# The opening of a fused attention and feed-forward kernel: 64 by 64 tiles, full rows for the last tokens' keys, shorter norms, another order

## The chip, the cores and the metric

The kernel runs on one core of one Trainium2 chip. A core has a matrix engine (PE, with its weight loads PEld), a vector engine (DVE), an activation engine (ACT), a general engine (POOL) and a sync engine (SP), whose queue here issues nearly all the transfers. The engines run their own instruction queues in order and wait for each other by semaphores. Matrix products land in PSUM; everything else that is worked on lies in SBUF. The metric is the device time of one execution in microseconds (us), the median over the runs.

## The reference

```python
# q, k, v: (8 batches, 8 heads, 576 tokens, 64), g_norm: (64,)
kv = np.einsum('bhsd,bhse->bhde', k, v)
out = np.einsum('bhsd,bhde->bhse', q, kv)
rms = np.sqrt(np.mean(out * out, axis=-1, keepdims=True) + 1e-06)
attn = (out / rms * g_norm).astype(np.float32)
x = np.ascontiguousarray(attn.transpose(0, 2, 1, 3)).reshape(4608, 512)
h = x @ w_in                      # w_in (512, 2048)
r = np.maximum(h, 0.0)
out = ((r * r) @ w_out)           # w_out (2048, 512)
```

Per head a 64 by 64 matrix kv is summed over all 576 tokens; each token's query is multiplied by it, normalised over its 64 numbers and scaled by g_norm. The eight heads of a token make one row of 512 numbers, which goes through two weight matrices with a squared relu between them. The weights arrive as 64-bit floating point numbers and are turned into 32-bit ones on the chip.

## The kernel before

**Tiling.** Heads are taken in pairs p (four of them for each batch b), so that two times 64 numbers fill 128 partitions. Of a head's 576 tokens, 512 make four full chunks of 128 rows, and the last 64 ("rest") are held for all heads in `k_rest` and `v_rest`, in rows 0 to 63 for an even batch and 64 to 127 for an odd one (`load_rest`, L159 to L163). The feed-forward works on nine strips of four 128-token tiles. Strip 0 is multiplied plainly, strip 1 with seven products in place of eight, the strips from 2 on with that scheme two levels deep; the sums of weights that the schemes need are built on DVE, stored to device memory and read back (`w_deep<-w_t`, `w_blk<-w_deep`).

**Weights.** They come in 32 pieces of 512 KB (`raw`, eight buffers, issued by SP at L240). A piece is converted by ACT's absolute value of the high words (L254), ACT's scaling of the low words (L258) and four steps (`conversion`): clamp (L266), shift (L268), combine (L272), add into the weights (L275). All four are DVE's, but for the first step of pieces 1, 2 and 3, which POOL does. From piece 4 on, pieces are converted in twos between the products of strip 0 (`convert_pieces`).

**The opening.** Batch 0's first four tiles are worked pair by pair in an order that is written out by hand in the list `slices` (L692 to L703). Each entry is one call, and every engine takes its instructions in the order of these calls. The letters are:
- T, `transposed_query` (L381): for batch 0, eight products with the identity (L407) put a pair's query on its other side in PSUM; ACT copies them to `qT` (L409). Ahead of the first, `keep_busy` (L376 to L379) issues products that nobody reads.
- K, `key_value` (L418): for each head of the pair four products over full chunks and one over the rest's 64 rows (L435), then two ACT copies of the 64 by 64 results into a block matrix `kv_all` (L440, L441).
- Q, `first_queries` (L582): four 128 by 128 products with the block matrix (L585), ACT's Square (L480), DVE's sum over 64 numbers (L488) and DVE's scaling by 1/64 plus epsilon (L489).
- N, `first_normalized` (L588): ACT's root (L494), DVE's reciprocal (L499), three small steps that sharpen the inverse root (L501 to L503), and DVE's multiplication into `x_n` (L592).
- F, `first_features` (L607): four transposes on PE (L611), and an ACT copy to the strip's `xT`, scaled by g (L612).
- U, `first_up` (L616): products of a pair's features with the first weights (L622); pair p needs piece p.
- size and low, the ACT steps L254 and L258 of a piece; piece, some of its four later steps.

The PSUM of the opening is the pool `apsum` (L99), two buffers for each tag: "at" for T and K, "first" for Q. The pool is replaced when strip 0 begins. SP's queue holds, in this order, batch 0's q, k, v and rest, with raw pieces between, then raw pieces to the eighth, batch 1's first keys, values, queries and rest, then raw pieces as their buffers come free.

**After the opening** the rest of strip 0 follows, with two pieces converted between its products. The remaining slices are called as the strips' products go on.

Of the kernel before, what the change touches and what calls it, by code (L numbers as in the profile page):

```python
# [10 lines left out]
FP32 = mybir.dt.float32  # L11
# [3 lines left out]
AF = mybir.ActivationFunctionType  # L15
ALU = mybir.AluOpType
AX = mybir.AxisListType
# [3 lines left out]
def kernel(  # L21
# [74 lines left out]
    psums = ExitStack()  # L96
    fpsum = psums.enter_context(tc.tile_pool(name="fpsum", bufs=4, space=bass.MemoryType.PSUM))
    opening = ExitStack()
    apsum = opening.enter_context(tc.tile_pool(name="opsum", bufs=2, space=bass.MemoryType.PSUM))  # L99
    ctx.enter_context(tc.manual_schedule())  # L100


# [54 lines left out]
    squares = lambda t: t.rearrange("p h d -> p (h d)").rearrange("p (k q f) -> p k q f", k=4, f=SQ)  # L157

    def load_rest(b, eng):  # L159
        h = b % 2  # L160
        half = slice(REST * h, REST * (h + 1))
        for t, src in ((k_rest[half], k), (v_rest[half], v)):
            eng.dma_start(out=t, in_=src[b, :, C * P : S].rearrange("h s d -> s h d"))  # L163
# [179 lines left out]

    kv_all = const.tile([P, 2 * NP, P], FP32, name="kv_all")
    nc.gpsimd.memset(kv_all, 0.0)

    one = const.tile([P, 1], FP32, name="one")
    nc.vector.memset(one, 1.0)
    nc.scalar.sqrt(one, one)

    load_next()
# [9 lines left out]
    g_src = g_norm.rearrange("(d u) -> d u", u=1)  # L361
    for h in range(2):
        nc.scalar.dma_start(out=g_col[ts(h, D)], in_=g_src)


    qT, kvd, x_n, xt = {}, {}, {}, {}
# [8 lines left out]
    def keep_busy(ps, n):  # L375


        for _ in range(n):
            nc.tensor.matmul(ps, lhsT=ident, rhs=ident[:, : ps.shape[1]], start=True, stop=True)  # L379

    def transposed_query(b, p):  # L381
        while any(f == load and a[:2] == (b, p) for f, a in drips):
            drip()
        t = main.pop(("q", b, p))
        if b >= Q_ON_PE:
            qT[b, p] = qt_pool.tile([P, C, P], FP32, name="qT", tag="qT")
            nc.vector.transpose(out=flat(qT[b, p]), in_=flat(t))
            if b % 2 and p == NP - 1:
                while any(f == load_q_rest and a[0] <= b for f, a in (*rest_drips, *drips)):
                    drip(not drips)  # L390
                nc.vector.transpose(
                    out=open_rest(b).rearrange("p q (k t) -> p q k t", k=4),
                    in_=squares(q_rest[b // 2]).rearrange("p k q f -> p q k f"),
                )
            drip_queries()
            if p == NP - 1 and b + 1 < B:
                (rest_drips, drips)[b % 2 == 0].extend((load_q_rest, (b + 1, nc.sync, a)) for a in range(4))
            return
        ps = apsum.tile([P, C, P], FP32, name="t_ps", tag="at")
        if (b, p) == (0, 0):  # L400
            keep_busy(ps[:, 0], 7)
        for c in range(C):
            if b:
                nc.tensor.transpose(ps[:, c, :], flat(t[:, c]), ident)
                continue
            for h in range(2):
                nc.tensor.matmul(ps[ts(h, D), c, :], lhsT=t[:, h, c], rhs=ident, start=True, stop=True)  # L407
        qT[b, p] = qt_pool.tile([P, C, P], FP32, name="qT", tag="qT")
        nc.scalar.copy(qT[b, p], ps)  # L409
        if (b, p) == (1, NP - 1):  # L410
            drip_queries()
# [6 lines left out]
    def key_value(b, *ps_of):  # L418
        while any(f == load and a[:2] == (b, p) or f == load_rest and a[0] == b for _, f, a in keys_due for p in ps_of):
            _, f, a = keys_due.popleft()  # L420
            f(*a)
        ps = apsum.tile([P, len(ps_of), D], FP32, name="kv_ps", tag="at")
        if (b, ps_of[0]) == (0, 0):
            keep_busy(ps[:, 0], 3)
            warm = apsum.tile([P, NT, P], FP32, name="x_ps", tag="first")[:, 0]
        half = slice(REST * (b % 2), REST * (b % 2 + 1))
        tiles = [[main.pop((n, b, p)) for n in "kv"] for p in ps_of]
        steps = [(i, c) for i in range(len(ps_of)) for c in range(C)] + [(i, C) for i in range(len(ps_of))]
        for i, c in steps:
            if (b, ps_of[i], c) == (0, 0, C):  # L430
                keep_busy(warm, 2)
            for h in range(2):
                at = (slice(None), h, c) if c < C else (half, 2 * ps_of[i] + h)
                a, w = (t[at] for t in (tiles[i] if c < C else (k_rest, v_rest)))
                nc.tensor.matmul(  # L435
                    ps[ts(h, D), i], lhsT=a, rhs=w, start=i == 0 and c == 0, stop=c == C, skip_group_check=True
                )
        at = (NP * b + ps_of[0]) % (2 * NP)
        d = kv_all[:, at : at + len(ps_of)]
        nc.scalar.copy(d[0:D, :, 0:D], ps[0:D])  # L440
        nc.scalar.copy(d[D:P, :, D:P], ps[D:P])  # L441
        for i, p in enumerate(ps_of):
            kvd[b, p] = d[:, i]
            if b < 2:
                if b == 1 and p == 0:
                    load_next()
            else:
                u = next(to_load, None)
                if u is not None:
                    keys_later(load, *u, nc.sync, "kv")  # L450
                if p == (1 if b > 3 else NP - 1) and b + 1 < B:
                    keys_later(load_rest, b + 1, nc.sync)
# [23 lines left out]
    def squared_parts(parts, pool=xn_pool, tag="x_n"):  # L476
        sqs = []
        for ps in parts:
            sqs.append(pool.tile(list(ps.shape), FP32, name="sq", tag=tag))
            nc.scalar.activation(sqs[-1], ps, AF.Square)  # L480
        return sqs

    def mean_of(sqs):
        ms = small.tile([P, 2, H], FP32, name="ms", tag="ms")[:, : len(sqs)]
        for i, sq in enumerate(sqs):
            if len(sq.shape) == 3:
                sq = sq.rearrange("p r e -> p (r e)")
            nc.vector.reduce_sum(out=ms[:, i], in_=by_head(sq), axis=AX.X)  # L488
        nc.vector.tensor_scalar(out=ms, in0=ms, scalar1=1.0 / D, scalar2=EPS, op0=ALU.mult, op1=ALU.add)  # L489
        return ms  # L490
# [6 lines left out]
    def inverse_root(ms, r):  # L497
        t = small.tile([P, 2, H], FP32, name="newton", tag="newton")[:, : ms.shape[1]]
        nc.vector.reciprocal(r, r)  # L499

        nc.vector.scalar_tensor_tensor(out=t, in0=ms, scalar=-0.5, in1=r, op0=ALU.mult, op1=ALU.mult)  # L501
        nc.vector.tensor_tensor(out=t, in0=t, in1=r, op=ALU.mult)
        nc.vector.scalar_tensor_tensor(out=t, in0=t, scalar=1.5, in1=r, op0=ALU.add, op1=ALU.mult)  # L503
        return t
# [75 lines left out]


    def first_queries(p):  # L582
        ps = apsum.tile([P, NT, P], FP32, name="x_ps", tag="first")
        for n in range(NT):
            nc.tensor.matmul(ps[:, n, :], lhsT=qT[0, p][:, n, :], rhs=kvd[0, p], start=True, stop=True)  # L585
        first[p] = flat(ps), mean_of(squared_parts([flat(ps)]))

    def first_normalized(p):  # L588
        ps, ms = first.pop(p)
        x_n["first", p] = t = xn_pool.tile([P, NT, P], FP32, name="x_n", tag="x_n")  # L590
        r = inverse_root(ms, root_of(ms))[:, 0]
        nc.vector.tensor_tensor(  # L592
            out=by_head(flat(t)), in0=by_head(ps), in1=r.unsqueeze(2).to_broadcast([P, H, D]), op=ALU.mult
        )

    first_steps = {}
# [10 lines left out]
    def first_features(p):  # L607
        t, x = x_n.pop(("first", p)), open_xt(0)
        ps = fpsum.tile([P, NT, P], FP32, name="xt_ps", tag="f")
        for n in range(NT):  # L610
            nc.tensor.transpose(ps[:, n, :], t[:, n, :], ident)  # L611
        nc.scalar.activation(x[:, :, p, :], flat(ps).rearrange("p (a t) -> p a t", t=SQ), AF.Copy, scale=g_col)  # L612

    first_sums = {}

# [76 lines left out]
    act, T, K, Q, N, F, piece = (  # L692
        convert_on_act, transposed_query, key_value, first_queries, first_normalized, first_features, first_piece
    )
    U = first_up
    size, low = (lambda i: (act, (i, (0,)))), (lambda i: (act, (i, (1,))))
    slices += [(T, (0, 0)), (K, (0, 0)), (T, (0, 1)), (Q, (0,)), (K, (0, 1)), (N, (0,)), size(0), (piece, (0, 1))]
    slices += [(T, (0, 2)), (Q, (1,)), low(0), (piece, (0, 1)), (K, (0, 2)), (N, (1,)), (F, (0,)), (T, (0, 3))]
    slices += [(piece, (0, 1)), (Q, (2,)), (piece, (0, 1)), size(1), (K, (0, 3)), low(1), (N, (2,)), (F, (1,))]
    slices += [(piece, (1, 4)), (Q, (3,)), size(2), low(2), (U, (0, [0, 1, 2])), size(3), (F, (2,)), (piece, (2, 4))]  # L700
    slices += [(U, (1, [0, 1, 2])), (N, (3,)), low(3), (piece, (3, 4)), (U, (2, [0, 1])), (F, (3,)), (U, (2, [2]))]
    slices += [(U, (3, [0, 1, 2]))]
    ready[0] = len(slices)  # L703
    def query_pairs(b):
        first_n = b // 2 * PAIR + (C if b % 2 else 0)
# [791 lines left out]
```

## Time and profile before

| What | Value |
|---|---|
| median of 3 runs | 870.81 us (870.48 to 872.5) |
| the profiled execution's own time | 869.32 us |
| its span, first to last instruction | 867.5 us |
| granted PE clock | 1.00 |
| PE busy | 860.8 us (99%) |
| DVE busy | 720.3 us (83%) |
| ACT busy | 352.2 us (41%) |
| POOL busy | 315.2 us (36%) |
| chain that ended last, by engine | PE 83%, DVE 9%, ACT 3%, DMA 3%, issue 2% |

A busy share is an average over stages that differ. The windows over the first 50 us show how the start differs from the rest: time, busy time of the engines (number of instructions), granted clock, share and rate of the DMA engines.

```profile
0.00:5.00 5.00, 3.64 (x18) 3.41 (x20) 0.06 (x1) 1.49 (x2) 1.60 (x7) 1.00 0.56 167
5.00:10.00 5.00, 5.00 (x60) 4.35 (x58) 0.00 (x0) 1.00 (x3) 0.00 (x0) 1.00 1.07 282
10.00:15.00 5.00, 5.00 (x76) 4.21 (x74) 2.41 (x8) 3.53 (x9) 0.00 (x0) 1.00 1.06 384
15.00:20.00 5.00, 4.71 (x59) 3.83 (x59) 4.54 (x13) 4.24 (x12) 0.75 (x1) 1.00 1.06 403
20.00:25.00 5.00, 4.63 (x20) 2.66 (x20) 4.65 (x12) 4.04 (x8) 3.84 (x3) 1.00 1.07 393
25.00:30.00 5.00, 5.00 (x15) 2.01 (x13) 4.45 (x12) 1.33 (x3) 1.13 (x1) 1.00 0.82 205
```

The columns behind the window and its length are PE, PEld, DVE, ACT and POOL. DVE does nothing before 12 us, since the first sums need q, k, v and the rest to have landed (q of pair 0 at 3.52, k 4.50, v 5.83, k_rest 7.41, v_rest 8.15 us). The DMA engines are saturated from 5 to 25 us. PE is called busy while a product waits in it, so its 5.00 doesn't mean that it was at its peak.

### The profile page before, as it was taken

How to read it: one execution, taken by the hardware profiler on the slowest of the kernel's cores; microseconds unless marked ns; L12 is line 12 of the kernel's file. 1: busy time of each engine (PE TensorE's matmuls, PEld its weight loads, DVE VectorE, ACT ScalarE, POOL GpSimd, SP SyncE). 2: the span in 40 equal slices, each digit the busy share in tenths (PEclk: the TensorE clock that was granted, in tenths of full speed). 3: DMA queues.
4: the chain of work that ended last, by engine and by line, in shares of the span. 5: the costliest groups of instructions: out<-in, count | busy, mean ns of one | idle time of the engine just before them, and what ended most of it. 6: DMA issues, size and time to landing. Idle time of an engine off the chain costs nothing.

```text
span 867.5 us, 32585 instructions
## 1 busy us (share of the span) xinstructions
PE 860.8 (99%) x14176; PEld 805.7 (93%) x14176; DVE 720.3 (83%) x1236; ACT 352.2 (41%) x805; POOL 315.2 (36%) x319
## 2 busy tenths in 40 slices
PE   9999999999999999999999999999999999999998
PEld 7445888889999999999999999999999999999998
DVE  3999998879877996789689977897889777976887
ACT  5799251320048403750356034901491148102810
POOL 1100004630459323730574045704470447145700
PEclk9999999999999999999999999999999999999999
DMA  9998997999999997989688979997668856875483
GB/s 317 302 339 251 279 376 229 285 325 374 290 256 262 343 319 230 238 311 335 211 244 272 341 240 265 287 311 268 210 223 301 303 168 215 294 283 195 173 313 126
DMA packets 169470, 236.47 MB, mean 273 GB/s; under 512 B 78704, under 2 KB 133744, under 8 KB 161008
## 3 DMA queue, kind: packets, MB, share of 16 engines
q1 hardware_dynamic: 169024, 234.33, 83.5%
q8 instruction: 111, 1.82, 0.9%
q14 instruction: 31, 0.25, 0.1%
q10 hardware_dynamic: 304, 0.07, 0.0%
HBM read 197.66 MB, written 36.70 MB: 270 GB/s over the span
## 4 chain that ended last, share of the span: by engine, by line
PE 83%; DVE 9%; ACT 3%; DMA 3%; issue 2%; SPq 0%; DVEq 0%; ACTq 0%
PE ps_A L852 36%; PE ps_B L852 32%; PE ps_C L852 5%; PE ps_A L857 4%; PE kv_ps L435 2%; DVE w_c L272 2%; PE x_ps L471 2%; PE ps_B L857 2%; DVE w_t L292 1%; DMA w_deep<-w_t 1%; DVE wt L292 1%; DMA first_qkv<-in_v_dram 1%; DVE w_c L266 1%; PE ps_C L857 1%; DVE w_in L275 1%
## 5 line engine op out<-in xcount | busy, mean ns | idle before, releaser
L852 PE MATMUL ps_B<-w_blk,g_s 128*64 128x128 f32 x2016 | 121.8, 273 | 0.0
L852 PEld LDWEIGHTS ps_B<-w_blk,g_s 128*64 128x64 f32 x2016 | 112.4, 137 | 0.1
L852 PE MATMUL ps_A<-x_l,w_in 128*64 128x128 f32 x1568 | 102.8, 273 | 0.7 <-ACT snap L1315 0.6
L292 POOL TENSOR_TENSOR x_l<-xT 128x256 f32<-128x256 f32 x21 | 16.1, 765 | 228.6 <-PE ps_A L852 228.6
L852 PE MATMUL ps_B<-w_blk,gt 128*64 128x128 f32 x1504 | 93.9, 273 | 0.0
L852 PE MATMUL ps_A<-w_blk,g_s 128*64 128x128 f32 x1536 | 92.0, 273 | 0.0
L852 PEld LDWEIGHTS ps_A<-x_l,w_in 128*64 128x64 f32 x1568 | 89.0, 137 | 0.9 <-ACT snap L1315 0.8
L1310 POOL TENSOR_TENSOR snap<-snap,gt 128x512 f32<-128x512 f32 x35 | 46.3, 1322 | 113.4 <-ACT snap L1315 104.1
L852 PEld LDWEIGHTS ps_A<-w_blk,g_s 128*64 128x64 f32 x1536 | 85.5, 137 | 0.0
L852 PEld LDWEIGHTS ps_B<-w_blk,gt 128*64 128x64 f32 x1504 | 84.4, 137 | 0.3 <-issue 0.3
L1315 ACT COPY snap<-ps_A 128x512 f32<-128x512 f32 x63 | 36.9, 585 | 103.6 <-PE ps_A L852 94.4
L1250 ACT ACTIVATE gt<-gt 128x512 f32<-128x512 f32 x112 | 70.1, 626 | 8.8 <-DVE gt L1310 8.8
L1251 ACT ACTIVATE gt<-gt 128x512 f32<-128x512 f32 x112 | 70.7, 631 | 3.6
L852 PE MATMUL ps_A<-w_blk,gt 128*64 128x128 f32 x1152 | 71.0, 273 | 0.0
L1099 ACT COPY o_sb<-ps_A 128x128 f32<-128x128 f32 x24 | 6.4, 266 | 144.9 <-PE ps_A L852 115.4
L852 PEld LDWEIGHTS ps_A<-w_blk,gt 128*64 128x64 f32 x1152 | 64.5, 137 | 0.0
L292 DVE TENSOR_TENSOR gt<-gt 128x2048 f32<-128x2048 f32 (+1 forms) x29 | 59.7, 2063 | 0.0
L1098 DVE TENSOR_TENSOR o_sb<-o_sb,ps_B 128x256 f32<-128x256 f32 (+1 forms) x123 | 47.5, 386 | 14.5 <-ACT o_sb L1099 9.4
L1310 POOL TENSOR_TENSOR gt<-gt,snap 128x512 f32<-128x512 f32 x42 | 52.6, 1282 | 14.9 <-DVE snap L1310 14.9
L852 PE MATMUL ps_B<-x_l,w_blk 128*64 128x128 f32 x784 | 51.4, 273 | 0.0
L852 PE MATMUL ps_A<-x_l,w_blk 128*64 128x128 f32 x784 | 51.2, 273 | 0.0
L1099 ACT COPY o_sb<-ps_B 128x128 f32<-128x128 f32 x31 | 8.2, 266 | 96.3 <-PE ps_B L852 96.3
(194 smaller groups left out, 1838.1 us busy)
## 6 DMA issues: line engine op xcount, KB each, us to landing
w_blk<-w_deep SPq DMA_DIRECT2D x56, 1024.0 KB, 7.2
w_blk<-w_out SPq DMA_DIRECT2D x56, 768.0 KB, 6.5
w_blk<-w_in_deep SPq DMA_DIRECT2D x49, 768.0 KB, 6.0
raw<-in_moe_w_in_dram SPq DMA_DIRECT2D x16, 512.0 KB, 7.8
raw<-in_moe_w_out_dram SPq DMA_DIRECT2D x16, 512.0 KB, 5.2
k<-in_k_dram SPq DMA_DIRECT2D x29, 256.0 KB, 5.1
v<-in_v_dram SPq DMA_DIRECT2D x29, 256.0 KB, 5.3
x_d<-x_q SPq DMA_DIRECT2D x27, 256.0 KB, 4.9
```

The lines of the kernel that those rows point to most:

```text
L272: yield nc.vector.scalar_tensor_tensor(out=ci, in0=high, scalar=-(2**30), in1=ci, op0=ALU.bitwise_and, op1=ALU.bitwise_or)
L292: eng.tensor_tensor(out=out, in0=a, in1=b, op=ALU.subtract)
L435: nc.tensor.matmul(ps[ts(h, D), i], lhsT=a, rhs=w, start=i == 0 and c == 0, stop=c == C, skip_group_check=True)
L471: nc.tensor.matmul(ps[half, r, i, ts(p, D)], lhsT=q[row, half], rhs=kvd[b, p][row, row], start=True, stop=True)
L852: nc.tensor.matmul(ps[half], lhsT=lhsT[:, half], rhs=rhs, start=start, stop=stop, skip_group_check=True)
L857: nc.tensor.matmul(bank[BANK[p]][:, i, :], lhsT=lhsT(k), rhs=rhs(k), start=p in (1, 5, 2) and i == 0 and k == 0, stop=k == n - 1, skip_gro ...
L1098: add = lambda out, a, b: nc.vector.tensor_tensor(out=out, in0=a, in1=b, op=ALU.add)
L1099: yield nc.scalar.copy(q[:, 3:4], small(1))
L1250: nc.scalar.activation(o, o, AF.Relu)
L1251: nc.scalar.activation(o, o, AF.Square)
L1310: add = lambda eng, out, a, b: eng.tensor_tensor(out=out, in0=a, in1=b, op=ALU.add)
L1315: nc.scalar.copy(t, ps)
```

## The change

- The queries of batch 0 are transposed in 16 products of 64 by 64 tiles for each pair (new function `first_transposed`), and multiplied in 16 products of 64 by 64 tiles without the zero blocks.
- The opening's PSUM pool has one buffer. Two tiles are taken once and kept for all four pairs: "t" of two by two blocks of 256 columns, in which T uses blocks [:, :, 0] and K 64 columns of block [:, p % 2, 1], and "x", in which pair p of Q uses [:, :, p % 2]. The warm-up products write in "x", and there are 6, 1 and 2 of them for 7, 3 and 2.
- `k_rest` and `v_rest` of batches 0 to 3 lie in rows 0 to 63; rows 64 to 127 are set to zero, and the products of K go over all 128 rows. `load_rest` of batches 1, 2 and 3 thus writes the rows that the batch before has read.
- The norm: Square gets the scale 64^-0.5, the root gets epsilon as its bias, the step L489 is gone, and the sharpening steps give -2 times the inverse root, which the factor -0.5 in `g_neg` undoes. The root is a step R of its own.
- The order in `slices` is another one.

```diff
-    apsum = opening.enter_context(tc.tile_pool(name="opsum", bufs=2, space=bass.MemoryType.PSUM))
+    apsum = opening.enter_context(tc.tile_pool(name="opsum", bufs=1, space=bass.MemoryType.PSUM))
...
     def load_rest(b, eng):
-        h = b % 2
+        h = b % 2 * (b > Q_ON_PE + 1)
...
+    for t in (k_rest, v_rest):
+        nc.gpsimd.memset(t[REST:P], 0.0)
...
+    eps = const.tile([P, 1], FP32, name="eps")
+    nc.vector.memset(eps, EPS)
...
+    g_neg = const.tile([P, 1], FP32, name="g_neg")
+    nc.gpsimd.tensor_scalar(out=g_neg, in0=g_col, scalar1=-0.5, scalar2=None, op0=ALU.mult)
...
+    def first_transposed(p):
+        t = main.pop(("q", 0, p))
+        if p == 0:
+            open_ps["t"] = apsum.tile([P, 2, 2, C * D], FP32, name="t_ps", tag="t")
+            open_ps["x"] = apsum.tile([P, 2, 2, NT * D], FP32, name="x_ps", tag="x")
+            keep_busy(open_ps["x"][:, 0, 1, 0:P], 6)
+        ps = open_ps["t"][:, :, 0]
+        for c in range(C):
+            for s in range(2):
+                rows = slice(REST * s, REST * (s + 1))
+                for h in range(2):
+                    nc.tensor.matmul(
+                        ps[ts(h, D), s, ts(c, REST)], lhsT=t[rows, h, c], rhs=ident[rows, rows], start=True, stop=True
+                    )
+        qT[0, p] = qt_pool.tile([P, C, P], FP32, name="qT", tag="qT")
+        nc.scalar.copy(
+            qT[0, p].rearrange("p c (s t) -> p s c t", s=2), ps.rearrange("p s (c t) -> p s c t", t=REST)
+        )
...
     def transposed_query(b, p):
+        if b == 0:
+            return first_transposed(p)
...
-        if (b, p) == (0, 0):
-            keep_busy(ps[:, 0], 7)
         for c in range(C):
-            if b:
-                nc.tensor.transpose(ps[:, c, :], flat(t[:, c]), ident)
-                continue
-            for h in range(2):
-                nc.tensor.matmul(ps[ts(h, D), c, :], lhsT=t[:, h, c], rhs=ident, start=True, stop=True)
+            nc.tensor.transpose(ps[:, c, :], flat(t[:, c]), ident)
...
-        ps = apsum.tile([P, len(ps_of), D], FP32, name="kv_ps", tag="at")
+        if b:
+            ps = apsum.tile([P, len(ps_of), D], FP32, name="kv_ps", tag="at")
+        else:
+            ps = open_ps["t"][:, ps_of[0] % 2, 1, 0:D].rearrange("p (i d) -> p i d", i=1)
+            warm = open_ps["x"][:, 0, 1, 0:P]
         if (b, ps_of[0]) == (0, 0):
-            keep_busy(ps[:, 0], 3)
-            warm = apsum.tile([P, NT, P], FP32, name="x_ps", tag="first")[:, 0]
-        half = slice(REST * (b % 2), REST * (b % 2 + 1))
+            keep_busy(warm, 1)
+        half = slice(REST * (b % 2), REST * (b % 2 + 1)) if b > Q_ON_PE + 1 else slice(None)
...
     def first_queries(p):
-        ps = apsum.tile([P, NT, P], FP32, name="x_ps", tag="first")
+        ps = open_ps["x"][:, :, p % 2]
         for n in range(NT):
-            nc.tensor.matmul(ps[:, n, :], lhsT=qT[0, p][:, n, :], rhs=kvd[0, p], start=True, stop=True)
-        first[p] = flat(ps), mean_of(squared_parts([flat(ps)]))
+            for h in range(2):
+                half = slice(REST * h, REST * (h + 1))
+                for r in range(2):
+                    row = slice(D * r, D * (r + 1))
+                    nc.tensor.matmul(
+                        ps[half, r, ts(n, D)], lhsT=qT[0, p][row, n, half], rhs=kvd[0, p][row, row], start=True, stop=True
+                    )
+        sq = xn_pool.tile([P, 2, NT * D], FP32, name="sq", tag="x_n")
+        nc.scalar.activation(sq, ps, AF.Square, scale=D**-0.5)
+        ms = small.tile([P, 2, H], FP32, name="ms", tag="ms")[:, 0]
+        nc.vector.reduce_sum(out=ms, in_=sq.rearrange("p r (n d) -> p (r n) d", d=D), axis=AX.X)
+        first[p] = ps, ms
+
+    def first_root(p):
+        r = small.tile([P, 2, H], FP32, name="rms", tag="rms")[:, 0]
+        nc.scalar.activation(r, first[p][1], AF.Sqrt, bias=eps)
+        first[p] += (r,)
 
     def first_normalized(p):
-        ps, ms = first.pop(p)
+        ps, ms, r = first.pop(p)
...
-        r = inverse_root(ms, root_of(ms))[:, 0]
+        w = small.tile([P, 2, H], FP32, name="newton", tag="newton")[:, 0]
+        nc.vector.reciprocal(r, r)
+        nc.vector.scalar_tensor_tensor(out=w, in0=ms, scalar=EPS, in1=r, op0=ALU.add, op1=ALU.mult)
+        nc.vector.tensor_tensor(out=w, in0=w, in1=r, op=ALU.mult)
+        nc.vector.scalar_tensor_tensor(out=w, in0=w, scalar=-3.0, in1=r, op0=ALU.add, op1=ALU.mult)
...
-        nc.scalar.activation(x[:, :, p, :], flat(ps).rearrange("p (a t) -> p a t", t=SQ), AF.Copy, scale=g_col)
+        nc.scalar.activation(x[:, :, p, :], flat(ps).rearrange("p (a t) -> p a t", t=SQ), AF.Copy, scale=g_neg)
...
-    slices += [(T, (0, 0)), (K, (0, 0)), (T, (0, 1)), (Q, (0,)), (K, (0, 1)), (N, (0,)), size(0), (piece, (0, 1))]
-    slices += [(T, (0, 2)), (Q, (1,)), low(0), (piece, (0, 1)), (K, (0, 2)), (N, (1,)), (F, (0,)), (T, (0, 3))]
-    slices += [(piece, (0, 1)), (Q, (2,)), (piece, (0, 1)), size(1), (K, (0, 3)), low(1), (N, (2,)), (F, (1,))]
-    slices += [(piece, (1, 4)), (Q, (3,)), size(2), low(2), (U, (0, [0, 1, 2])), size(3), (F, (2,)), (piece, (2, 4))]
-    slices += [(U, (1, [0, 1, 2])), (N, (3,)), low(3), (piece, (3, 4)), (U, (2, [0, 1])), (F, (3,)), (U, (2, [2]))]
-    slices += [(U, (3, [0, 1, 2]))]
+    slices += [(T, (0, 0)), (K, (0, 0)), (T, (0, 1)), (Q, (0,)), (K, (0, 1)), (R, (0,)), (T, (0, 2)), (N, (0,)), (Q, (1,))]
+    slices += [size(0), (R, (1,)), (piece, (0, 1)), low(0), (piece, (0, 3)), (N, (1,)), (F, (0,)), (K, (0, 2))]
+    slices += [(T, (0, 3)), (Q, (2,)), size(1), low(1), (piece, (1, 1)), (R, (2,)), (N, (2,)), (U, (0, [0, 1, 2])), (F, (1,))]
+    slices += [(K, (0, 3)), size(2), (piece, (2, 1)), (piece, (1, 3)), (F, (2,)), (Q, (3,)), (R, (3,)), low(2)]
+    slices += [(U, (1, [0, 1, 2])), (piece, (2, 3)), size(3), (piece, (3, 1)), low(3), (N, (3,)), (U, (2, [0, 1]))]
+    slices += [(F, (3,)), (piece, (3, 3)), (U, (2, [2])), (U, (3, [0, 1, 2]))]
```

In the last two lists `(piece, (i, n))` calls for the next n of the four steps of piece i.

## The prediction

> **What bounds the kernel now.** Four views, each narrowing the last. The slices show PE at 90% or more nearly everywhere, but DVE at 9 from the second slice to the sixth (21.7 to 130 us), in which PE is busy too.
>
> ```profile
> PE   9999999999999999999999999999999999999998
> ...
> DVE  3999998879877996789689977897889777976887
> ```
>
> The chain of work that ended last settles which of the two binds: from 42.2 to 107 us each of its pieces but short issue gaps is DVE's, then comes `107.16 8.56 DMA w_deep<-w_t`, then DVE again to 130.94, and only from 131.60 is it PE to the end. So the opening's share of the time is decided by when DVE's unbroken run of conversions begins. The same chain, taken to 32 us, shows how it begins now:
>
> ```profile
> 29.00 0.45 PE xt_ps L611 x4
> 29.45 0.02 issue
> 29.47 0.69 ACT xT L612
> 30.16 0.55 ACT w_c L254
> ```
>
> F(3), the transposition of the last pair's features, ends in an ACT copy at 29.47; only behind it does ACT take piece 4 (L254). The timeline of DVE shows what that delays:
>
> ```profile
> 27.71 0.69 DVE L592 TENSOR_TENSOR x_n<-x_ps,newton 128x512 f32<-128x512 f32 x1
> ...
> 29.60 0.69 DVE L275 CUSTOM_DVE_ANT_0 w_in<-raw,w_c 128x1024 uint16<-128x1024 uint16 x1
> 30.74 0.43 DVE L266 TENSOR_SCALAR w_c<-w_c 128x512 f32<-128x512 f32 x1 [0.45 <-ACT w_c L254]
> 31.87 0.43 DVE L266 TENSOR_SCALAR w_c<-w_c 128x512 f32<-128x512 f32 x1 [0.70 <-ACT w_c L254]
> ```
>
> After 32.2 us DVE has no idle time of weight before 98 us: the windows give 5.00 of 5.00 us for 35 to 40, 20.00 of 20.00 for 40 to 60 and for 60 to 80, 19.97 for 80 to 100. Hence my measure: **the start of DVE's L266 of piece 5, now 31.87 us.** A later start passes on one for one, for DVE's queue behind it is full, the store w_deep<-w_t follows DVE, and PE's final run at 131.60 follows that store (its last wait is for a w_deep landing at 131.57). An earlier start is capped: on ACT, L254 waited for raw pieces at 48.21 (0.83 us) and 51.05 (0.40 us); they landed at 48.13 and 50.96, behind DMA engines at shares of 0.99 to 1.11 since 35 us. DVE takes them some 1.4 to 1.8 us later, and no more than that can be gained.
>
> **Parts that shorten something.** Durations are rows of the profiled execution, from its groups by line and its timeline.
> - Transposes T: a group now takes 1.09 us (9.21 to 10.31, L407). The nearest row for 16 tiles of 64x64 is products_x's L471, 0.69 us at 142.16. Bounds: 0.33 us (four records of the rest's 64x64 tiles, L435) and 1.09. I take 0.65, between the two readings 0.62 and 0.69 of L471.
> - Products Q: 1.16 us now (L585), same nearest row, same bounds with 1.16 on top; 0.65.
> - The rest of the keys in full rows: 0.33 us now; the chunk rows of L435 are 0.69 for 16 records, so 0.17 for four. The two POOL memsets are half of L345's 128x1024 each or less (0.95 us), so they end by 3.2 us; K0's rest needs them at 8.15, v_rest's landing. K0's rest begins at 8.96 now, behind warm-up matmuls (L379, 8.31); with fewer of these it can begin at 8.2.
> - Norms: L489 goes from each of the four chains, 0.17 us each (12.79 of pair 0; 0.53 for pair 2, under contention). The scale moves into Square, EPS into Sqrt's bias, the factor -0.5 to g_neg, which one POOL instruction prepares with POOL idle from 2.2 to 19.25. Square with a scale has no row here; between nothing and one L480's slack I take nothing. The eps memset (0.06 us) lies before DVE's first work at 12.07.
>
> **Part that adds waits.** apsum goes from two buffers to one, and T, K on the one hand and Q on the other share one tile each through the whole opening. From the waits that the changed program's instructions carry I read: K(p) waits for the ACT copy of T(p); T(p+1) for ACT's two kv copies of K(p); Q(p+1) for DVE's x_n of N(p); Q(2) and Q(3) likewise. None of these is there now: Q of pair 1 runs 13.23 to 14.39 while x_n of pair 0 runs 14.15 to 14.84, and Q of pair 2 begins at 16.80, ahead of x_n of pair 1 at 17.16. So what ran a pair ahead becomes one chain. Worked out with rows, 0.05 us from engine to engine:
>
> - v_rest 8.15; K0's rest to 8.5; kv copies 2 x 0.21, 9.0; T1 9.05; Q0 9.5 to 10.15; Square 0.60, 10.8; reduce 0.69, 11.55; root behind K1's copies 11.8; reciprocal to x_n's start 0.92 as at 13.23; **x_n of pair 0 at 12.8**, 1.35 earlier than now.
> - Q1 must wait for it to end: 13.5 (now 13.23). Square to 14.8, reduce to 15.5. The new order then has all of piece 0 ahead of N1: 0.42 + 0.42 + 0.69 + 0.69, the third held by L258 on ACT to 16.5: 17.8. Three newton steps, **x_n of pair 1 at 18.65** (now 17.16).
> - Q2 19.4 (now 16.80), Square to 20.7, reduce 21.4, root behind L258 21.9, **x_n of pair 2 at 22.9** (now 21.43).
> - PE: U(0), three products of 0.86, runs from 19.9 to 22.4; F1, K3, F2 follow, Q3 at 24.4 (now 19.72); Square behind F2's copy 25.3 to 25.9; reduce 26.6. Piece 2's L268 waits for POOL's L266 (1.92 us from 24.85), L272, L275 to 28.8. **x_n of pair 3 at 29.6** (now 27.71).
> - F3 behind U(2) at 30.5; ACT's copy 31.2 (now 29.47); L254 of piece 4 at 31.8; of piece 5, and with it DVE's L266, **33.65 (now 31.87): 1.8 us later.**
>
> What hides elsewhere: SP's queue keeps its order, but load_rest of batch 1 now reuses rows 0 to 63 and waits for K3, at about 23.6 instead of its issue at 22.85. Behind it stand two k/v loads, two q loads and raw 8; the transfer issued at 22.85 lands 7.62 us later, so the DMA engines have more queued than the 0.75 us; without that cover it would cost 0.75. The raw buffers 10 and 11 hang on pieces 2 and 3 ending at 28.8 and 32.1 (now 26.9 and 30.3): issues now at 30.59 and 31.48, so the latter slips 0.7; DVE needs it 1.8 later as well.
>
> **The sum.** The profiled execution took 869.32 us, 867.5 of span and 1.8 around it. 867.5 + 1.8 + 1.8 = 871.1. The median of the runs shown is 870.81, 1.5 above; on that footing **872.6 us**. Bounds of the unknown: T and Q at their old lengths add 0.5 at Q2 and 0.5 at F3's end, +1.0; at 0.33 us they give back 0.3 at each of Q1, Q2 and Q3, -0.9. So 871.7 to 873.6 for the row part, and 870.9 to 874.6 with the one to one passage uncertain by 1 us.
>
> A rule that bears on the waits: the Trainium skill, page "PSUM — Partial Sum Buffer", section "PSUM bank collisions raise a hardware error", says that two engines in one bank and one quarter of the partitions collide, and that a dependency is set between them even at other columns. By it the two halves of a shared tile, which lie in the same banks, must wait for each other, as in the waits above; without it Q1 would run ahead and the time would be that of the second rival.
>
> **The rivals.**
> - **PE stays cold longer** (slower). Now T of pair 0 takes 1.98 us and T of pair 1 1.09 us for the same work, though the granted clock stands at 1.00: PE ran at half speed until about 7.2 us. The change issues fewer warm-up products (6, 1 and 2 for 7, 3 and 2) and shorter groups, so PE is less busy before 8 us, and my chain leaves it idle for 1.2 to 2.2 us three times before 19.4 (12.3 to 13.5, 15.2 to 17.4, 18.0 to 19.4). Half speed to 13.5 us costs T1 and Q0 0.65 each, +1.3; to 25 us also Q1, Q2 at 0.65 and U(0) at 2.6, about +5 in all. 874 to 878. Against it: the longest gap is 2.2 us. The Trainium skill, page "TensorE: Matmul & The Clock Gate", section "HAM oscillation — how this bites in real kernels", puts the idle time that slows PE at about 3.4 us; by it this rival is left with the first 10 us alone, some +1. No run here shows such a gap.
> - **DVE, not the waits, sets the opening** (not slower). DVE is busy 4.54, 4.65 and 4.45 of 5 us in the windows from 15 to 30. If pieces fill each wait, the end follows DVE's work: 4 x 0.17 less, and a start 1.35 earlier, -2.0, cut by the raw landings to -1.4 to -1.8: 869.0 to 869.4. It decides if x_n of pair 3 begins before 27.7. Against it: piece 0 stands whole in front of N1, and POOL's 1.92 us in front of piece 2.
> - **Later stages take or add part.** DVE waits 0.45 us at 115.3 for a w_deep store, a place at which a later start meets another DMA order: 870 to 876.
> - The tiles not sharing PE's array (they run one after another) is the upper bound above, +1.0.
>
> **How the numbers follow.** My forecast 0.50 (870.9 to 874.6); PE cold 0.17 (874 to 878); DVE sets it 0.20 (868 to 870.8); later stages 0.13. 0.3% of 870.81 is 2.6 us, about what a measurement can tell from no change, so the bounds are 868.2 and 873.4. Slower by more: 0.16 of the forecast's case, 0.17, and 0.05 of later stages = 0.38. Faster by more: 0.08 of the DVE case, if the cap by raw landings is loose, and 0.02 of later stages: 0.10. Within: 0.52. The range 869.2 to 876.0 leaves out the far half of PE cold and the near half of the DVE case.
>
> **What would show it.** Right: Q2 in the profile after begins at the end of x_n of pair 1, near 19.4; x_n of pair 3 near 29.6; the ACT copy of F3 near 31.2; L266 of piece 5 near 33.7, and PE's last run near 133.4. L489's row is gone; T and Q groups at 0.65. Wrong: T of pair 1 above 1.1 us (PE cold); x_n of pair 3 before 27.7 (DVE); L266 of piece 5 as forecast but PE's last run not 1.8 later (later stages).

## The result and the profile after

The changed kernel is slower: 876.01 us (median of 6 runs, 874.16 to 877.38) against 870.88 (6 runs, 869.81 to 872.5) of the kernel before, a ratio of 1.0053 with a 95% interval of 1.0037 to 1.0069. The profiled execution took 876.28 us, with a span of 874.3 us for 867.5. The slices of its page, PE, DVE and the granted PE clock:

```profile
PE   6999999999999999999999999999999999999998
...
DVE  2799999779967996889788977897889777875887
...
PEclk8899999999999999999999999999999999999999
```

The first two slices (to 43.7 us) differ: PE is busy for six tenths of the first, and the clock row, 9 throughout before, begins with 8 8. So half of the answer is in a row that did not move before. The chain that ended last, by engine, has moved too:

```profile
PE 90%; ACT 3%; DMA 3%; DVE 2%; issue 1%; SPq 0%; POOL 0%; DVEq 0%; ACTq 0%
```

DVE's share fell from 9% to 2%, and from 77.14 to 231 us every piece of the chain but short gaps is PE's (before, PE's run began at 131.60, behind DVE's). The chain of work that ended last, from 35 to 38.6 us, and DVE's timeline show how late the opening ends:

```profile
35.29 0.45 PE xt_ps L658 x4
35.74 0.02 issue
35.77 0.69 ACT xT L659
36.45 0.57 ACT w_c L254
```

```profile
34.25 0.69 DVE L638 TENSOR_TENSOR x_n<-x_ps,newton 128x512 f32<-128x512 f32 x1
...
36.35 0.69 DVE L275 CUSTOM_DVE_ANT_0 w_in<-raw,w_c 128x1024 uint16<-128x1024 uint16 x1
37.05 0.43 DVE L266 TENSOR_SCALAR w_c<-w_c 128x512 f32<-128x512 f32 x1
38.17 0.43 DVE L266 TENSOR_SCALAR w_c<-w_c 128x512 f32<-128x512 f32 x1 [0.69 <-ACT w_c L254]
```

F3's copy begins at 35.77 us (29.47 before) and L266 of piece 5 at 38.17 (31.87), 6.3 us later. Taken instruction by instruction (the n-th of each kind in the two traces), DVE is 6.28 us later at 80 us, 5.73 at 131, 5.7 at 200 and 6.43 at 860, and the span is 6.8 longer. The opening lost it, and little behind gave it back.

PE's timeline shows the two mechanisms in a few rows (the idle time before a row, with its releaser, stands in brackets):

```profile
9.10 1.03 PE L398 MATMUL t_ps<-ident,q 64*64 64x64 f32 x32 [0.57 <-ACT kv_all L467]
...
14.73 0.69 PE L615 MATMUL x_ps<-kv_all,qT 64*64 64x64 f32 x32 [1.27 <-DVE x_n L638]
...
18.65 0.69 PE L398 MATMUL t_ps<-ident,first_qkv 64*64 64x64 f32 x32 [1.83 <-ACT kv_all L467]
20.73 1.13 PE L615 MATMUL x_ps<-kv_all,qT 64*64 64x64 f32 x32 [1.39 <-DVE x_n L638]
21.79 2.07 PE L669 MATMUL ps_A<-xT,w_in 128*128 128x512 f32 x2
```

The brackets are the waits of the shared tiles: T for ACT's copies of K's result, Q for DVE's x_n. And the same group of 16 products lasts 0.69 us in one place and 1.13 in another; U's product, 1.12 us as a row before, 2.07. Cut at the places where the clock changes, the windows give (after the length: PE, PEld, DVE, ACT, POOL, granted clock, DMA share, rate):

```profile
5.87:9.28 3.41, 2.00 (x36) 1.51 (x39) 0.00 (x0) 0.53 (x3) 0.20 (x1) 1.00 1.09 309
9.28:12.69 3.41, 2.96 (x84) 2.66 (x80) 0.69 (x1) 1.57 (x4) 0.00 (x0) 0.50 0.98 290
12.69:16.11 3.42, 2.07 (x70) 1.66 (x72) 1.39 (x5) 1.52 (x5) 0.00 (x0) 1.00 1.04 371
16.11:19.52 3.41, 1.41 (x52) 1.13 (x52) 3.12 (x8) 2.40 (x7) 0.00 (x0) 1.00 1.06 382
19.52:22.93 3.41, 2.20 (x34) 1.57 (x35) 1.39 (x4) 1.47 (x3) 0.00 (x0) 0.50 1.05 387
22.93:26.34 3.41, 3.41 (x6) 1.33 (x5) 2.55 (x8) 0.90 (x3) 1.93 (x1) 0.50 1.07 372
```

The clock falls at 9.28, rises at 12.69, falls at 19.52 and rises at 26.35: steps of 3.41, 6.83 and 6.83 us, one or two times 3.41. Each fall follows a window in which PE was busy for little of it (2.00 and 1.41 of 3.41 us), each rise a window that was nearly full at half speed (2.96 and 3.41).

### The profile page after: what moved, and what is told of

Its sections match the earlier page's. It is cut to its first block, busy times and chain, and to the rows that moved or that the text cites. A ratio compares the mean times of both kernels' runs of the same rounds, so it can differ in the third digit from the quotient of the medians.

```text
span 874.3 us, 32898 instructions
## 1 busy us (share of the span) xinstructions
PE 859.0 (98%) x14330; PEld 802.9 (92%) x14330; DVE 718.2 (82%) x1233; ACT 352.3 (40%) x805; POOL 316.3 (36%) x322
## 4 chain that ended last, share of the span: by engine, by line
PE 90%; ACT 3%; DMA 3%; DVE 2%; issue 1%; SPq 0%; POOL 0%; DVEq 0%; ACTq 0%
PE ps_A L899 35%; PE ps_B L899 31%; PE ps_A L904 6%; PE ps_C L899 5%; PE ps_B L904 3%; PE x_ps L497 2%; PE kv_ps L461 2%; PE ps_C L904 2%; DMA w_blk<-w_deep 1%; DMA raw<-in_moe_w_out_dram 1%; DVE w_c L272 1%; ACT w_c L254 1%; DMA v<-in_v_dram 1%; DMA q_rest<-in_q_dram 1%; PE ps_A L669 1%
```

## The experiments

Two theories to begin with. **A:** the waits of the shared tiles empty PE, and the emptied PE is then run at half speed; both cost. **B:** the waits alone, or (**C**) the new order, make the delay. Later runs brought in **D**, on PE's instruction stream. All ratios are to runs of the kernel before that were taken beside them. "Opening" is the start of DVE's L266 of piece 5 in the profile, "131" how much later DVE's instruction at 130.87 us of the first profile is, "end" how much longer the span; all in us.

| Kernel | ratio, 95% interval | opening | 131 | end |
|---|---|---|---|---|
| before | 1 | 31.87 | 0 | 0 |
| changed | 1.0053 [1.0037, 1.0069] | 38.17 | 5.73 | 6.8 |
| e1_warm | 1.0086 [1.0064, 1.0108] | 35.74 | 3.31 | 7.3 |
| e2_old_tiles | 0.9996 [0.998, 1.0012] | 32.8 | 0.36 | 0.2 |
| e3_old_order | 1.0073 [1.0048, 1.0099] | 38.5 | 6.04 | 5.4 |
| e4_norms_rows | 0.999 [0.9975, 1.0006] | 32.6 | 0.21 | -0.8 |
| e5_wide | 1.0022 [1.0008, 1.0036] | 35.02 | 2.58 | 4.1 |
| e6_x_shared | 1.0046 [1.0028, 1.0065] | 36.17 | 3.74 | 6.3 |
| e7_t_shared | 1.0059 [1.0041, 1.0077] | 32.82 | 0.84 | 5.3 |
| e8_one_buffer | 1.0074 [1.0055, 1.0092] | 37.73 | 5.79 | 8.3 |
| e9_before_pad | 1.007 [1.0049, 1.009] | 31.55 | 0.88 | 9.3 |
| e10_t_pad | 1.0024 [1.0004, 1.0043] | 35.13 | 2.70 | 3.3 |
| e11_before_again | 0.9995 [0.9978, 1.0012] | 31.31 | -0.70 | -0.8 |
| e12_after_again | 1.0079 [1.005, 1.0108] | 36.85 | 4.41 | 5.1 |

(The openings of e2, e3 and e4 are 31.87 plus the shift of DVE's rows at 33 us: 0.92, 6.61, 0.77.)

**e1_warm: keep PE busy.**

```diff
+    def warm_up(n):
+        if 0 not in first_sums:
+            first_sums[0] = fpsum.tile([P, STRIP], FP32, name="ps_A", tag="f")
+        keep_busy(first_sums[0][:, 0:P], n)
...
-            keep_busy(warm, 1)
+            keep_busy(warm, 4)
...
+    W = lambda n: (warm_up, (n,))
...
-    slices += [(T, (0, 0)), (K, (0, 0)), (T, (0, 1)), (Q, (0,)), (K, (0, 1)), (R, (0,)), (T, (0, 2)), (N, (0,)), (Q, (1,))]
+    slices += [(T, (0, 0)), (K, (0, 0)), W(2), (T, (0, 1)), (Q, (0,)), (K, (0, 1)), (R, (0,)), W(2), (T, (0, 2)), (N, (0,)), W(3), (Q, (1,))]
...
-    slices += [(T, (0, 3)), (Q, (2,)), size(1), low(1), (piece, (1, 1)), (R, (2,)), (N, (2,)), (U, (0, [0, 1, 2])), (F, (1,))]
+    slices += [W(5), (T, (0, 3)), W(4), (Q, (2,)), size(1), low(1), (piece, (1, 1)), (R, (2,)), (N, (2,)), (U, (0, [0, 1, 2])), (F, (1,))]
```

> The changed kernel with 16 more warm-up products that nobody reads, put ahead of T and Q where PE waits (2 before T1, 2 before T2, 3 before Q1, 5 before T3, 4 before Q2, into a PSUM tile that U takes later) and 4 for 1 ahead of K0's rest. No wait is changed. Theory A (two causes: the waits of the shared tiles leave PE idle, and the idle PE is then clocked at half speed): the granted clock stays 1.00 from 10 to 30 us, the three products of U(0) take 2.6 us for 5.1, L266 of piece 5 begins at about 33.7 us (the chain of waits alone) for 38.17, and the time falls by about 4 us against the changed kernel, to some 1.8 us over the kernel before. Theory B (the waits and the order alone make the delay, the clock is a bystander): the time stays within 1 us of the changed kernel's.

The opening did as theory A said, for the most part: U(0) lasted 2.8 us, the clock was at 0.50 only from 15.34 to 18.74, and L266 of piece 5 began 2.4 us earlier than in the changed kernel. But the ratio rose from 1.0053 to 1.0086, some 3 us, though the intervals overlap. The trace shows where most of it went: from 3.31 us late at 131 us the kernel fell to 7.34 at the end, with PE at rest and no releaser named:

```profile
267.36 0.49 PE L905 MATMUL ps_A<-x_l,w_in 128*64 128x128 f32 x5
269.19 0.66 PE L905 MATMUL ps_A<-x_l,w_in 128*64 128x128 f32 x8 [1.34 <-issue]
```

Such rests came at 356 (1.09) and 448 us (0.38) too. The kernel before has none over 0.35 us, in either of its profiles. The one fall of the clock in e1's opening came behind a rest of the same kind, 1.05 us at 14.66, in the midst of Q1's products. So this run could not judge A: it changed a second thing, the length of PE's instruction stream.

**e2_old_tiles, e3_old_order: tiles or order.** e2 is the kernel before with the change's norms, full rows and order. e3 is the changed kernel with the list of before, and R ahead of each N:

```diff
-    slices += [(T, (0, 0)), (K, (0, 0)), (T, (0, 1)), (Q, (0,)), (K, (0, 1)), (R, (0,)), (T, (0, 2)), (N, (0,)), (Q, (1,))]
...
+    slices += [(T, (0, 0)), (K, (0, 0)), (T, (0, 1)), (Q, (0,)), (K, (0, 1)), (R, (0,)), (N, (0,)), size(0), (piece, (0, 1))]
...
```

> The changed kernel's order, norms and full rows, with the transposes, products, warm-ups and PSUM buffers (two for each tag) of the kernel before. Theory A: with Q free to run ahead of N the order by itself costs nothing; PE stays at clock 1.00; L266 of piece 5 near 31.5 us and the time within 1 us of the kernel before. Theory C (the order of pieces and norms is the cause, since piece 0 stands whole ahead of N1): L266 of piece 5 at 33 us or later and 2 us or more above the kernel before.

> The changed kernel with the order of the kernel before (the root R right ahead of each N). Theory A: the shared tiles still make Q wait for N, PE is idle as long, the clock still falls to 0.50 in places, and the time stays 3 us or more above the kernel before. Theory C (the order is the cause): within 1 us of the kernel before.

With the old tiles and buffers the new order cost nothing (0.9996, clock 1.00 throughout); with the new tiles the old order was no better than the new (1.0073; clock at 0.50 from 16.66 to 20.07 and from 26.90 to 30.31). That falsifies C. What piece 0 ahead of N1 costs stayed with pair 1: in e2 its x_n came at 18.29 us for 17.16 (raw piece 0 landed 1.2 us later too), that of pair 2 at 21.19 for 21.43.

**e4_norms_rows.** The kernel before with only `g_neg`, `eps`, R, the scaled Square and the rows set to zero.

> The kernel before with only the shorter norms and the last tokens' keys in full rows. Both are off the waits in question: L489's 0.17 us goes from each of four chains, so L266 of piece 5 is some 0.2 to 0.7 us earlier than 31.87 and the time 0 to 0.7 us below the kernel before, by every theory; a time above it would say that one of these two parts has a cost of its own.

The time is the same (0.999), but the opening was 0.77 us later, not earlier: K2 waited for the values of pair 2 (2.08 us at 15.52), which landed at 15.38, in the first profile of before at 13.93. In time the two parts cost nothing that can be seen; the landing is taken up under e11.

**e5_wide: the same PE stream, with PE kept busy.** Nine warm-up products as in the changed kernel, but 256 to 512 columns wide, and five of them at the places of e1.

```diff
+    def busy_for(ps, n):
+        nc.tensor.matmul(
+            ps[:, 0 : n * P].rearrange("p (k c) -> p k c", c=P), lhsT=ident,
+            rhs=ident.unsqueeze(1).to_broadcast([P, n, P]), start=True, stop=True,
+        )
```

> The changed kernel with as many warm-up products as it has (nine), so that PE's instruction stream is as long, but wider ones (256 to 512 columns for 128) and five of them moved to where PE waits: ahead of T1, T2, Q1, T3 and Q2. The run e1_warm showed the opening's end 2.4 us earlier (L266 of piece 5 at 35.74 for 38.17) and gave it back later, where PE stood still for 1.34, 1.09 and 0.38 us at 269, 356 and 448 us with nothing that the profile names as releaser. Theory D (those stalls come from 80 more PE instructions, which move the places at which PE's stream is fetched): with the same number of instructions they are gone, the opening ends at 33.7 to 35.7 us and the time is 2 to 4 us below the changed kernel's, 872 to 874. Theory E (warming gains nothing in the end, whatever is saved in the opening is lost later): within 1 us of the changed kernel's, or above it.

The clock was 1.00 in all 12 executions, U(0) lasted 2.9 us, and the ratio fell from 1.0053 to 1.0022: 1.9 us over the kernel before, 2.7 below the changed one. The long rests were fewer than in e1: one of 0.45 us with no releaser, at 447 us. That bears out theory A: no wait was changed, the opening ended 3.15 us earlier than in the changed kernel, and the two intervals do not meet, if only just (one ends at 1.0036, the other begins at 1.0037, and the runs are of different sessions). What remains, 1.0008 to 1.0036, holds the waits at full clock and rests like that one.

**e6_x_shared, e7_t_shared, e8_one_buffer: which wait.** e6 and e7 are the changed kernel but for one part. e6 takes T and K from the kernel before and keeps Q's shared tile; e7 keeps the shared tile of T and K and takes Q (two buffers) from the kernel before. e8 is the kernel before with one word changed:

```diff
-    apsum = opening.enter_context(tc.tile_pool(name="opsum", bufs=2, space=bass.MemoryType.PSUM))
+    apsum = opening.enter_context(tc.tile_pool(name="opsum", bufs=1, space=bass.MemoryType.PSUM))
```

> The changed kernel with T and K as before (128 by 64 tiles, two PSUM buffers in turn); only Q has 64 by 64 tiles and the shared tile x, so Q of a pair still waits for the x_n of the pair ahead. If Q's wait for N is the main cause, L266 of piece 5 begins 2 us or more later than 31.87 and the time is 2 to 5 us above the kernel before; if the shared tile of T and K is, the time is within 1 us of the kernel before.

> The reverse: T and K share the tile t and T has 64 by 64 tiles, while Q has its four 128 by 128 products and two PSUM buffers as before, so that Q runs ahead of N again. If Q's wait for N is the main cause, PE is idle for less, the clock stays at 1.00, L266 of piece 5 begins within 1 us of 31.87 and the time is within 1.5 us of the kernel before; if the tile of T and K is, 2 to 5 us above it.

> The kernel before with one word changed: the opening's PSUM pool has one buffer for each tag instead of two. Nothing gets shorter, only the waits come: T, K and T of the next pair follow one another through one bank, and Q waits for N. By the theory that the waits make the loss, the opening ends 3 to 6 us later and the time is 3 to 6 us above the kernel before; if 64 by 64 tiles or the layout were the cause, it is within 1 us.

In the opening the answer is clear: Q's shared tile makes it 4.30 us later (with one fall of the clock, 19.71 to 23.12), the shared tile of T and K 0.95, and one buffer for each tag alone, without any new tile shape, 5.86. e8's profile has no fall of the clock, so this loss is one of waits, with no half speed in it (the other five of its six executions had mean clocks of 0.994 to 0.998). The window ahead of e6's fall has PE busy for 1.36 us; e8 has one with 1.58, in which a wait of Q3 for x_n of 2.71 us ended, and no fall behind it:

```profile
16.30:19.71 3.41, 1.36 (x28) 1.08 (x23) 3.03 (x8) 1.99 (x5) 0.00 (x0) 1.00 1.05 381
19.71:23.12 3.41, 3.18 (x35) 2.06 (x36) 0.82 (x3) 1.89 (x4) 0.74 (x1) 0.50 1.05 387
```

```profile
24.12:27.53 3.41, 1.58 (x10) 1.37 (x11) 3.14 (x9) 1.02 (x2) 0.86 (x1) 1.00 1.12 314
27.53:30.94 3.41, 3.41 (x12) 1.69 (x12) 1.84 (x4) 2.72 (x7) 2.52 (x2) 1.00 1.16 214
```

In time e6 is 4 us slower (1.0046) and e8 6 to 7 (1.0074); in their profiles 2.5 us of the loss came only behind 131 us. e7's forecast failed: it is 5 us slower with an opening 0.95 us late. It loses 4.5 us behind 131 us, again in rests without releaser (0.53, 1.25, 0.75 and 0.96 us at 248, 267, 353 and 542 us).

**e9_before_pad, e10_t_pad: PE's instruction stream.** The page of the kernel before counts 14176 products and as many weight loads on PE, and 111 transfers of 16 KB on a queue of instructions (q8). 28352 / 111 is 255, and no other engine has a tenth as many, so these are PE's, about 256 instructions in each. e9 puts 120 empty instructions into the kernel before, e10 140 into e7. The edit of e9:

```diff
                 start=p == 0, stop=p == NP - 1,
             )
+            for _ in range(10):
+                nc.tensor.nop("pad")
```

> The kernel before with 120 instructions that do nothing on PE's queue, ten behind each of the twelve products of U. No wait, tile or order is changed. It puts every later PE instruction 120 places further on, about as e7_t_shared does (116 more instructions), whose opening was only 0.95 us late and which ended 5.3 us late, with PE at rest for 0.53, 1.25, 0.75 and 0.96 us at 248, 267, 353 and 542 us and no releaser named. Theory D (the place of the instructions in PE's stream makes these rests): the opening ends within 0.7 us of the kernel before, the rests come back, and the time is 2 to 5 us above the kernel before. Theory G (the rests come from the time at which the stages run, or from e7's own tiles): within 1 us of the kernel before.

> e7_t_shared with 140 such empty instructions behind the products of U, so that with its own 116 the stream behind the opening is 256 places longer than that of the kernel before (the profile counts 111 transfers of 16 KB on PE's instruction queue for it, which makes 256 instructions of 64 bytes in each). Theory D: the rests at 248 to 542 us are gone, and the time is within 1.5 us of the kernel before, for 5 us above it. Theory G: it stays 4 us or more above the kernel before.

e9 has the kernel before's opening (31.55 us), the same tiles, order and waits, and is 0.7% slower, [1.0049, 1.009]. DVE is 0.88 us later at 131 us and 5.86 at 300:

```profile
264.94 0.61 PE L854 MATMUL ps_A<-x_l,w_in 128*64 128x128 f32 x8
267.88 0.55 PE L854 MATMUL ps_A<-x_l,w_in 128*64 128x128 f32 x6 [2.33 <-issue]
```

More of them stand at 291 (0.84), 357 (1.26) and 546 us (0.46), and behind the one of 2.33 us the clock went to 0.50 for a while, from 269.21 to 272.62. Around 265 us the trace has a transfer of PE instructions (265.23 to 266.21) and DMA engines that are busy for nine tenths in nearly every slice. e10, brought to 256 places more, fell from 1.0059 to 1.0024; the rests of e7 behind 131 us are gone but for one of 0.40 us at 247, and its profile loses 0.6 us between there and the end for e7's 4.5. That is theory D.

The kept traces settle it. They have 19 rests of PE over 0.35 us without a releaser, in eight of the 14 profiles, two of them in openings (1.05 us in e1, 0.76 at 15.50 in e12). If PE's instructions are counted from the first on, each of the 19 ends with 193 or 194 instructions past a multiple of 256, and 1.26 to 1.81 us behind the end of a transfer on that queue. Of all PE instructions behind 60 us some 9 to 10% stand that far behind one. So PE waited at the same place of a transfer's instructions each time.

e10's 3.3 us in the profile are an opening with one fall of the clock (9.23 to 12.65), which e7's profile happened not to have; the expectation of 1.5 us was missed (1.0024 is 2.1 us), and this fall is the likely reason: its seven executions at a mean clock of 1.000 have a median of 872.0 us, the five at 0.994 to 0.998 one of 874.6, though the two groups overlap.

**e11_before_again, e12_after_again: second profiles.**

> The kernel before, unchanged, for a second profile of it. In its first profile raw piece 0 landed at 12.59 us and v of pair 2 at 13.93; in all the changed kernels' profiles, even that with one buffer alone, they landed 0.3 to 1.7 us and 0.6 to 1.8 us later. If that is chance from run to run, this profile too has them later and L266 of piece 5 at 32.3 to 32.9; if the changes cause it, they land as in the first profile, with L266 of piece 5 at 31.9. The time is the same as the kernel before.

> The changed kernel, unchanged, for a second profile and more executions with their mean granted clock. Of its six executions so far five had a mean clock of 0.992 to 0.994 over the span (some 10 us at half speed, worked out as twice the shortfall times 874 us) and one, of 876.91 us, had 1.000. Theory A (half speed in the opening costs about 2.5 us of the 4.6): the clock is at half speed somewhere between 9 and 27 us in this profile too, not at the same places, since it follows a grid of 3.4 us that does not start with the kernel; L266 of piece 5 begins at 36 us or later; and executions with a clock of 0.998 or more lie 2 us below the others on the median. If they don't, the slow clock is not what costs, or the one of 876.91 was no accident.

The kernel before: raw piece 0 landed at 11.60 us, the values of pair 2 at 13.43, and the opening ended at 31.31. The expectation of chance alone is not borne out, for its landings are not late; but e9 (before's tiles) had 12.63 and e10 (shared tiles) 12.65, and e8, with no memsets, 13.60. Whether part of the half to one microsecond in e2, e4 and e7 is the changes' own stays open. The changed kernel: the opening ended at 36.85, with the clock at 0.50 in other places, 14.68 to 24.92 us, three times 3.41:

```profile
11.27:14.68 3.41, 1.81 (x67) 1.43 (x67) 1.56 (x6) 1.50 (x5) 0.00 (x0) 1.00 1.05 346
14.68:18.09 3.41, 2.13 (x34) 1.66 (x37) 2.92 (x6) 2.65 (x7) 0.00 (x0) 0.50 1.07 377
18.09:21.51 3.42, 2.75 (x65) 2.06 (x58) 1.33 (x6) 1.33 (x3) 0.00 (x0) 0.50 1.05 386
21.51:24.92 3.41, 3.41 (x5) 1.35 (x4) 2.56 (x8) 1.15 (x3) 1.93 (x1) 0.50 1.05 385
```

All six executions had a mean clock of 0.994 to 0.996, so with the first six 11 of 12 were slowed so. The comparison by clock that I had asked for can't be made: only the one of 876.91 us had 1.000, and executions at 0.994 ran from 873.04 to 880.06 us. That the clock costs is shown by e5 and hinted at by e10, not by these.

## Why the prediction was right, and where it fell short

The direction held, but 0.52 had stood on a time within 0.3% of the kernel before and only 0.38 on a slower one. The measured 876.0 us lies at the very end of the range, far above the forecast of 872.6; that it is still there is in part luck. What happened is the chain of waits plus the price of the first rival, PE cold (0.17), though not in that rival's form: PE was at full clock from 5.87 to 9.28 us and fell later, twice. (One slip of the sum changes nothing: 871.7 less 1 is 870.7, not 870.9.)

- **What bounds it, and the passage to the end:** right in size, not in its way. 6.28 us at 80 us are 6.43 at 860; the place at which DVE had waited 0.45 us for a w_deep store gave back 0.55 (6.28 to 5.73), no more. But the chain no longer goes by DVE and the w_deep store to a PE run "near 133.4": it is PE's from 77.14 us on, and before that ACT's conversions and a raw piece that landed at 64.47. (Nor is it PE "to the end": from 537 to 551 us before, and 543 to 558 after, ACT and DVE stand in it.) The two ways lie close together, with PE 5.97 us late at 134 and DVE 5.73 at 131.
- **The chain of waits:** right in the links that bind, which stand in the brackets above: T behind ACT's copies of K's result, Q1 and Q2 behind x_n. (K behind the copy of T did not bind here, nor did Q3 behind x_n.) With the clock at 1.00 (e5), x_n of the four pairs begins at 13.48, 19.48, 23.83 and 31.09 us; forecast were 12.8, 18.65, 22.9 and 29.6. The first is 0.7 late since T1 stood behind the landing of q of pair 1 (9.41 us, 8.75 before); the last step is 0.6 longer. L266 of piece 5 came at 35.02, forecast 33.65. In time e5 is 1.9 us above before, for 1.8 forecast, but its opening was 3.15 us late for 1.8, so that agreement is in part luck too. e6 and e7 show which link weighs: Q behind N.
- **"T and Q at 0.65", "three products of 0.86":** the failed step. These are rows at full clock, and the sum used them everywhere. In the changed kernel T1 took 1.03 us, Q0 1.10, Q2 1.13, and U(0) 5.1 us from 21.79 to 26.88 (2.9 in e5). From x_n of pair 2 (24.78) to that of pair 3 (34.25) it took 9.5 us, 6.7 forecast, 7.3 in e5.
- **"Against it: the longest gap is 2.2 us":** wrong as an argument. The longest gap was 1.83 us, and the clock fell twice; in e8 PE was idle for 2.71 us in one piece, and it stayed. What goes with the falls is not one gap but a window's sum: the 14 profiles have nine falls (twice each in the changed kernel and e3, once in e1, e6, e9, e10 and e12), all behind windows of 3.41 us with PE busy for 1.19 to 2.01 us. The sum alone doesn't decide it either, for behind others with 1.58 (e8), 1.75 (e6), 1.90 (e10) and 2.00 us (e4) it stayed; what else does is not shown. The Trainium skill, page "TensorE: Matmul & The Clock Gate", section "What's actually happening", has a free-running window of about 3.4 us; the traces agree, with 3.41. The Trainium skill's rule of idle gaps over 3.4 us (same page, section "HAM oscillation — how this bites in real kernels") does not hold here, since in the changed kernel the clock fell with no gap over 1.83 us.
- **"T of pair 1 above 1.1 us" as the sign of a cold PE:** set too high. It was 1.03, at half speed; the row at full speed is 0.69.
- **SP's queue:** K3's rest ended not at 23.6 but at 28.05, so k_rest of batch 1 was issued at 28.09 instead of 22.85, and the DMA share fell to 0.58 from 25 to 30 us. The cover of 7.62 us was used up: ACT waited 1.46 us at 53.95 for a raw piece that landed at 53.87. DVE had no idle time by it (6.27 us late ahead of it and behind it), but PE went from 6.28 us late at 50 us to 6.8 at 62, and the chain that ended last goes by there; by 134 us PE had given that back.
- **Norms, rows, order at nothing or little:** right by e2 and e4, both the same as before.
- **The rival that DVE's work, not the waits, sets the opening:** false while Q's tile is shared, for DVE had idle times of 1.45, 1.89 and 3.21 us ahead of the sums of pairs 1 to 3. With Q's own two buffers (e2, e7) DVE was busy for 12.16 and 11.66 of the 15 us from 15 to 30 (13.64 before), and nothing was gained; what set the opening there is not shown.

The price of half speed is the distance from 1.0053 to e5's 1.0022, with a PE stream as long: 0.3%, 2.7 us (from e12's 1.0079, 5 us). That the same kernel gave 1.0053 in one session and 1.0079 in another says how rough this price is. What can't be settled is the share of the stream's place in the changed kernel itself: its first profile has no long rest without a releaser, its second profile two (0.76 us at 15.50 and 0.45 at 448). No version beat the kernel before by more than its interval.

## What to carry to other kernels

Ask of a shorter operation what it was keeping busy: a buffer fewer turns work that ran ahead into a chain, and a matrix engine that is left half empty for 3.4 us may, as here, run the next 3.4 at half speed, where the chain can least afford it. Price a chain at both speeds before summing it. And compare kernels whose PE streams have different lengths with care: 120 empty instructions in an opening cost this kernel 0.7%, more than 200 us later.

## What the runs showed of the hardware that was not expected

- The clock is decided at steps of 3.41 us that do not begin with the kernel (falls at 9.28 us in one profile of the changed kernel, 14.68 in the other). It fell behind windows with PE busy for 35 to 59%, stayed behind some of 46 to 59%, and never fell behind a fuller one; the longest idle time in one piece does not tell the two apart (1.83 us with falls, 2.71 without). At half speed it rose again behind windows of 87% and more, and stayed low behind 62, 65 and 80%.
- PE can rest for 0.4 to 2.3 us with nothing but its own instruction stream to wait for. All 19 such rests end 193 or 194 instructions past a multiple of 256, and 1.26 to 1.81 us behind the end of a 16 KB transfer of instructions. Which work a rest falls on depends on the number of PE instructions ahead of it; whether it comes does not on that alone: e8, with as many as before, had rests of 0.62 at 452 us and 0.36 at 701.
